# The experts' second product turned round: w2's tiles as weights, 512 tokens moving, gate weights at the relu

## The chip, the core and the metric

The kernel runs on one core of a Trainium2 chip. The metric is the device time of one execution in microseconds (us); a kernel's time is the median of its runs. Some executions also carry a profile, from which all durations below come.

## What is computed

Three networks follow each other. The first is a linear recurrence over 768 time steps (4 batches, 8 heads of 48 features); its output, as 3072 tokens of 384 features, is the x of a mixture of 8 experts. Its output in turn goes through a layer with h x cos(h).

```python
def _moe_ref(x, w_gate, w1, w2):          # N, D, E, F = 3072, 384, 8, 1024
    logits = x @ w_gate
    P = np.exp(logits - logits.max())
    for _ in range(8):
        P /= P.sum(1, keepdims=True) + 1e-09
        P /= P.sum(0, keepdims=True) + 1e-09
        P *= N / E
    out = np.zeros((N, D))
    for e in range(E):
        h = np.maximum(x @ w1[e], 0.0)
        out += P[:, e:e + 1] * (h @ w2[e])
    return out

def _moe2_ref(x, w_in, w_out):            # d_ff = 2048
    h = x @ w_in
    return (h * np.cos(h)) @ w_out
```

## The kernel before

**Units, blocks, steps.** Both dense networks are cut into units of 256 hidden columns (FU): four a expert (UPE), 32 for the experts (NU1), eight more for the second network (40, NU). The tokens are cut into six blocks of 512 (TB, NTB), a block into four tiles of 128 (TPB). One `step(u, tb)` does a unit for a block, in two halves f = 0, 1. Every value is split into a high and a low part (hh and hl, xh and xl, wh and wl), and a product is three matmuls, high x high, high x low and low x high (`three`, L288).

**g1 and g2.** `g1` (L340) makes a hidden tile of 128 hidden features by 512 tokens: three 128-deep slices of w1 are the weights, xh and xl of the block move, nine matmuls of 512 columns into a PSUM bank. `relu_split` (L293) writes hh with ScalarE and hl with VectorE, both from the bank. `g2` (L358) multiplies with w2: weights are 128 tokens of hh or hl, w2's 384 columns move; six matmuls give one token tile of 384 features. A half of a step holds one g1 and two g2 of the step before, by the queue `g2q`. `evac` (L320) adds the bank to the accumulator `acc`, which lies as token by feature; for experts 1 to 7 one VectorE operation multiplies by the token's gate weight P on the way (L326), for expert 0 (units 0 to 3), whose weight is not known yet, plain sums are kept and scaled in unit 4 by ScalarE (L370).

**Stages and order.** 24 chunks of attention come first (loop at L682), with units 0 and 1 laid between their parts as filler: each chunk pulls `one()` twice, and a pull is half of a step's half (a g1, or the g2's behind it). Then units 2 to 39 run. `gate_tasks` (L545) computes P beside units 0 to 3, one piece a pull; weights are loaded and split by `weight_tasks` (L275) the same way, with wl on GpSimd. `to_moe2` (L603) turns the accumulator into the second network's x beside units 31 and 32: four TensorE transposes into a bank, then ScalarE (xh) and VectorE (xl). PSUM has eight banks: two for g1 (`ps1`), two to five for g2 (`ps2`), and X0, X1, X2, used by attention, gate and transposes in turn; X0 and X1 join the rings at block 4 of unit 32. The order on each engine is that of the code; nothing reorders it.

Of the kernel before, what the change touches and what calls it, by code (L numbers as in the profile page):

```python
# [9 lines left out]
F32 = mybir.dt.float32  # L10
# [4 lines left out]
ALU = mybir.AluOpType  # L15
# [52 lines left out]
def setup(tc, ap, big, psp):  # L68
# [5 lines left out]
    def sb(name, cols, dt=F32):  # L74
        return big.tile([128, cols], dt, name=name)
# [9 lines left out]
    t.accb = [sb(f"acc{i}", TPB * DM) for i in range(NTB)]  # L85
    t.acc = [t.accb[i // TPB][:, i % TPB * DM:(i % TPB + 1) * DM] for i in range(NTT)]
# [21 lines left out]
    t.wp = sb("wp", 8 * HP)[0:112].rearrange("p (i j o) -> p i j o", i=8, o=1)  # L108
    t.ps = [psp.tile([128, 512], F32, name=f"ps{i}") for i in range(8)]
# [95 lines left out]
def body(tc, ap, t, fast, branch=None):  # L205
    nc = tc.nc
    te, act, dve, pool, sp = nc.tensor, nc.scalar, nc.vector, nc.gpsimd, nc.sync
    acc, P, xh, xl = t.acc, t.P, t.xh, t.xl
# [84 lines left out]
    def relu_split(ps, hh, hl):  # L293
        act.activation(out=hh, in_=ps, func=AF.Relu)  # L294
        dve.scalar_tensor_tensor(out=hl, in0=ps, scalar=0.0, in1=hh.bitcast(F32), op0=ALU.max, op1=ALU.subtract)  # L295
# [23 lines left out]

    def evac(u, tt, ps):  # L320
        if u == 0:
            act.activation(out=acc[tt], in_=ps, func=AF.Copy)
        elif u < UPE:
            dve.tensor_tensor(out=acc[tt], in0=ps, in1=acc[tt], op=ALU.add)
        elif u < NU1:
            dve.scalar_tensor_tensor(  # L326
                out=acc[tt], in0=ps, scalar=P[:, tt, u // UPE:u // UPE + 1], in1=acc[tt], op0=ALU.mult, op1=ALU.add)
        elif u == NU1:
            act.activation(out=acc[tt], in_=ps, func=AF.Copy, scale=TWO_PI)
        else:  # L330
            dve.scalar_tensor_tensor(  # L331
                out=acc[tt], in0=ps, scalar=TWO_PI, in1=acc[tt], op0=ALU.mult, op1=ALU.add)
            if u == NU - 1:
                sp.dma_start(out=ap["out"][tt * 128:(tt + 1) * 128, :], in_=acc[tt])
# [5 lines left out]
    def g1(u, tb, f):  # L340
        assert (u, 1) in wdone
        wh, wl = t.wh[u % 2], t.wl[u % 2]
        hh, hl = hid[u, tb, f] = hring.next()
        ps = ps1.next()
        for k in range(KT):
            o = k * FU + f * 128
            three(ps, wh[:, o:o + 128], wl[:, o:o + 128], xh[tb][:, k], xl[tb][:, k], k == 0, k == KT - 1)
        return (relu_split if u < NU1 else cos_split)(ps, hh, hl)
# [8 lines left out]

    def g2(u, tb, i):  # L358
        ps = ps2.next()[:, 0:DM]
        for f in range(2):  # L360
            g2_part(u, tb, i, f, ps)
        evac(u, tb * TPB + i, ps)

    def step(u, tb, lag=0):

        if u == UPE:
            assert not gq
            for i in range(TPB):
                tt = tb * TPB + i
                act.activation(out=acc[tt], in_=acc[tt], func=AF.Copy, scale=P[:, tt, 0:1])  # L370
        for f in range(2):
            rest = g1(u, tb, f)
            yield
            if len(g2q) > lag:
                a, b, i = g2q.popleft()
                g2(a, b, i)
                g2(a, b, i + 1)
            if rest:
                rest()
            if f == 1:  # L380
                g2q.extend([(u, tb, 0), (u, tb, 2)])
            yield
# [219 lines left out]

    def to_moe2(tb):  # L603

        yield
        for k in range(KT):
            ps = (X0, X1)[(tb * KT + k) % 2]
            for i in range(TPB):
                te.transpose(  # L609
                    ps[:, i * 128:(i + 1) * 128], acc[tb * TPB + i][:, k * 128:(k + 1) * 128], t.ident)  # L610
            act.activation(out=xh[tb][:, k], in_=ps, func=AF.Copy, scale=1.0 / TWO_PI)
            dve.scalar_tensor_tensor(  # L612
                out=xl[tb][:, k], in0=ps, scalar=1.0 / TWO_PI, in1=xh[tb][:, k].bitcast(F32),
                op0=ALU.mult, op1=ALU.subtract)
            yield
# [109 lines left out]
    for u in range(2, NU):  # L725
        if u == UPE:
            while gq:
                pull(gq)
            ps2.items.append(X2)
        for tb in range(NTB):  # L730
            if tb == (1 if u + 1 < NU1 else 0) and u + 1 < NU:
                wq.append(weight_tasks(u + 1))
            if u == NU1 - 1 and tb >= 2:
                xq.append(to_moe2(tb - 2))
            if u == NU1 and tb in (0, 2):
                xq.append(to_moe2(NTB - 2 + tb // 2))
            if u == NU1 and tb == 4:
                assert not xq
                ps1.items.append(X0)
                ps2.items.append(X1)  # L740
            dense.append(Step(u, tb, lag=1 if u >= NU1 else 0))
            while one():
                pass

    late.popleft()(True)
    u, tb, i = g2q.popleft()
    while len(g2q) >= 2:
        g2(u, tb, i)
        g2(u, tb, i + 1)
        u, tb, i = g2q.popleft()  # L750
# [8 lines left out]
def program(tc, ap):  # L759
    nc = tc.nc  # L760
    with ExitStack() as stack:
# [3 lines left out]
        t = setup(tc, ap, big, psp)  # L765
# [77 lines left out]
```

## Time and profile before

| | us |
|---|---|
| median of 3 runs (2151.34 to 2154.53) | 2152.92 |
| profiled execution, its own time | 2150.08 |
| its span | 2148.3 |
| TensorE busy | 2130.2 |
| VectorE busy | 1118.8 |
| ScalarE busy | 651.1 |
| GpSimd busy | 434.7 |

The profile names TensorE PE (its weight loads PEld), VectorE DVE, ScalarE ACT, GpSimd POOL, and SyncE's DMA queue SPq. The busy time of pipelined matmuls is modelled and runs over into the next; how fast TensorE goes is read from the distance between two starts. The granted clock was 0.996 of full speed over the span. Lines (L289) are those of the kernel before.

### The profile page before, as it was taken

Reading aid. Unit: us, or ns where it says so; the run is one execution under the profiler, and the core shown is the slowest. Engines: PE = TensorE matmul, PEld = TensorE weight load, DVE = VectorE, ACT = ScalarE, POOL = GpSimd, SP = SyncE. Lnnn points to the kernel's source line nnn. Section 1 sums busy time; section 2 is a strip of 40 time slices with the busy share of each in tenths; the row PEclk is TensorE's granted clock in tenths of the full one; section 3 lists DMA queues with packets and bytes.
Section 4 is the critical chain, followed back from the end, with each engine's and each line's share of the span. In section 5 each row is a group of like instructions: output and inputs, shape, how many; then the busy total and the mean of one; then the engine's idle time right before and its main releaser. Section 6 shows DMA issues by size and latency. Waiting matters only on the chain.

```text
span 2148.3 us, 29906 instructions
## 1 busy us (share of the span) xinstructions
PE 2130.2 (99%) x12229; PEld 1910.7 (89%) x12229; DVE 1118.8 (52%) x1980; ACT 651.1 (30%) x1246; POOL 434.7 (20%) x404
## 2 busy tenths in 40 slices
PE   8999999999999999999999999999999999999998
PEld 6887889999999999999999999999999989999998
DVE  8553654444444444444444444444444676777775
ACT  4553123111111111111111111111111267666664
POOL 8872000000000000000000000000000024444442
PEclk8999999999999999999999999999999999999999
DMA  7441000000000000000000000000000001110002
GB/s 227 135 143 36 23 15 15 15 16 19 19 19 19 15 16 15 16 15 16 15 15 16 15 19 19 16 19 19 16 15 23 23 23 33 35 30 30 30 23 91
DMA packets 37331, 70.79 MB, mean 33 GB/s; under 512 B 4416, under 2 KB 27328, under 8 KB 37184
## 3 DMA queue, kind: packets, MB, share of 16 engines
q1 hardware_dynamic: 37184, 68.78, 10.6%
q8 instruction: 98, 1.61, 0.3%
q14 instruction: 49, 0.40, 0.1%
HBM read 64.04 MB, written 4.72 MB: 32 GB/s over the span
## 4 chain that ended last, share of the span: by engine, by line
PE 97%; DVE 1%; DMA 1%; ACT 0%; issue 0%; SPq 0%; DVEq 0%
PE ps L289 31%; PE ps L291 31%; PE ps L290 31%; PE ps L461 1%; PE ps L502 1%; PE ps L510 1%; PE ps L528 0%; DMA raw<-in_rkT_dram 0%; PE ps L609 0%; DMA st<-in_wpk_dram 0%; PE ps L556 0%; PE ps L557 0%; DVE xl L612 0%; ACT raw L307 0%; ACT raw L308 0%
## 5 line engine op out<-in xcount | busy, mean ns | idle before, releaser
L295 DVE SCALAR_TENSOR_TENSOR hl<-ps,hh 128x512 fp32r<-128x512 f32 x384 | 266.1, 693 | 773.0 <-ACT hh L294 772.9
L289 PE MATMUL ps<-wh,hh 128*128 128x384 f32 x1920 | 649.4, 338 | 0.0
L291 PE MATMUL ps<-wh,hl 128*128 128x384 f32 x1920 | 647.8, 337 | 0.0
L290 PE MATMUL ps<-wl,hh 128*128 128x384 f32 x1920 | 644.9, 336 | 0.0
L294 ACT ACTIVATE hh<-ps 128x512 fp32r<-128x512 f32 x384 | 230.1, 599 | 1265.0 <-PE ps L291 1264.8
L291 PE MATMUL ps<-xh,wl 128*128 128x512 f32 x1440 | 569.5, 395 | 0.0
L290 PE MATMUL ps<-xl,wh 128*128 128x512 f32 x1440 | 568.3, 395 | 0.0
L289 PE MATMUL ps<-xh,wh 128*128 128x512 f32 x1440 | 564.3, 392 | 0.7 <-DVE raw L311 0.7
L326 DVE SCALAR_TENSOR_TENSOR acc<-ps,P,acc 128x384 f32<-128x384 f32 x672 | 410.9, 613 | 83.3 <-PE ps L291 83.3
L267 POOL TENSOR_TENSOR wl<-st,wh 128x384 fp32r<-128x384 f32 x120 | 121.8, 1015 | 1351.3 <-PE ps L291 1298.5
L289 PEld LDWEIGHTS ps<-wh,hh 128*128 128x128 f32 x1920 | 360.8, 188 | 21.4
L290 PEld LDWEIGHTS ps<-wl,hh 128*128 128x128 f32 x1920 | 360.5, 188 | 19.5
L291 PEld LDWEIGHTS ps<-wh,hl 128*128 128x128 f32 x1920 | 360.1, 188 | 0.0
L291 PEld LDWEIGHTS ps<-xh,wl 128*128 128x128 f32 x1440 | 270.0, 187 | 58.1
L289 PEld LDWEIGHTS ps<-xh,wh 128*128 128x128 f32 x1440 | 270.6, 188 | 48.3 <-issue 3.0
L290 PEld LDWEIGHTS ps<-xl,wh 128*128 128x128 f32 x1440 | 270.1, 188 | 45.2
L315 POOL TENSOR_TENSOR hl<-raw,hh 128x512 fp32r<-128x512 f32 x95 | 140.7, 1481 | 209.5 <-ACT hh L314 110.6
L304 DVE SCALAR_TENSOR_TENSOR raw<-raw,ps 128x512 f32<-128x512 f32 x96 | 66.0, 688 | 72.7 <-ACT raw L303 72.7
L303 ACT ACTIVATE raw<-ps,magic 128x512 f32<-128x512 f32 x96 | 66.1, 689 | 102.1 <-PE ps L291 100.8
L331 DVE SCALAR_TENSOR_TENSOR acc<-ps,acc 128x384 f32<-128x384 f32 x168 | 87.8, 551 | 4.9 <-PE ps L291 4.9
L311 DVE SCALAR_TENSOR_TENSOR raw<-raw,ps 128x512 f32<-128x512 f32 x96 | 66.0, 688 | 20.2 <-ACT raw L308 20.2
L307 ACT ACTIVATE raw<-raw 128x512 f32<-128x512 f32 x96 | 61.0, 636 | 24.9 <-DVE raw L304 24.9
(134 smaller groups left out, 1013.8 us busy)
## 6 DMA issues: line engine op xcount, KB each, us to landing
st<-in_wpk_dram SPq DMA_DIRECT2D x128, 192.0 KB, 2.4
AM<-in_wpk_dram SPq DMA_DIRECT2D x32, 384.0 KB, 3.0
raw<-in_rkT_dram SPq DMA_DIRECT2D x21, 448.0 KB, 3.6
kr<-in_kr_dram SPq DMA_DIRECT2D x21, 384.0 KB, 4.1
v<-in_v_dram SPq DMA_DIRECT2D x21, 224.0 KB, 4.5
out_dram<-acc SPq DMA_DIRECT2D x24, 192.0 KB, 1.9
acc<-in_rkT_dram SPq DMA_DIRECT2D x3, 448.0 KB, 3.9
acc<-in_kr_dram SPq DMA_DIRECT2D x3, 384.0 KB, 4.6
```

The costliest lines, as they stand in the source:

```text
L267: (dve if u < 2 else pool).tensor_tensor(out=wl[:, s], in0=src, in1=wh[:, s].bitcast(F32), op=ALU.subtract)
L289: te.matmul(ps, ah, bh, start=first, stop=False)
L290: te.matmul(ps, ah, bl, start=False, stop=False)
L291: te.matmul(ps, al, bh, start=False, stop=last)
L294: act.activation(out=hh, in_=ps, func=AF.Relu)
L295: dve.scalar_tensor_tensor(out=hl, in0=ps, scalar=0.0, in1=hh.bitcast(F32), op0=ALU.max, op1=ALU.subtract)
L303: act.activation(out=f, in_=ps, func=AF.Identity, bias=t.magic)
L304: dve.scalar_tensor_tensor(out=f, in0=f, scalar=MAGIC, in1=ps, op0=ALU.subtract, op1=ALU.subtract)
L311: dve.scalar_tensor_tensor(out=f, in0=f, scalar=0.5, in1=ps, op0=ALU.subtract, op1=ALU.mult)
L315: (dve if last else pool).tensor_tensor(out=hl, in0=f, in1=hh.bitcast(F32), op=ALU.subtract)
L326: dve.scalar_tensor_tensor(out=acc[tt], in0=ps, scalar=P[:, tt, u // UPE:u // UPE + 1], in1=acc[tt], op0=ALU.mult, op1=ALU.add)
L331: dve.scalar_tensor_tensor(out=acc[tt], in0=ps, scalar=TWO_PI, in1=acc[tt], op0=ALU.mult, op1=ALU.add)
```

## The change

Three things change. First, g2 for the experts becomes `g2T`: a 128x128 slice of w2 is the weight, hh and hl of the block move with 512 columns, and a bank holds 128 output features by 512 tokens. Three such products (k = 0, 1, 2) replace four, and they are queued as one in the first half and two in the second. The accumulator lies as feature by token (`accT`) until unit 32.

Second, a token's gate weight now differs along the columns. It is applied to the hidden tile: for experts 1 to 7 VectorE writes h = max(ps, 0) x pb, ScalarE copies it to hh, VectorE subtracts. `pb` holds an expert's gate weights of a block on all 128 partitions; P is transposed (two TensorE transposes), written to DRAM, and loaded back with broadcast, twelve loads ahead of unit 4 and six in each expert's last unit. Expert 0's sum is multiplied by `pb0` on GpSimd in unit 4.

Third, `to_moe2` needs no transposes, and X0, X1 and X2 join the rings at unit 4 (one more bank for g1, two for g2).

```diff
-    def relu_split(ps, hh, hl):
+    hring32 = Ring([x[:, 0:TB] for x in t.v[0:3]])
+    def relu_split(e, tb, ps, hh, hl):
+        if e:
+            h = hring32.next()
+            dve.scalar_tensor_tensor(out=h, in0=ps, scalar=0.0, in1=t.pb[tb], op0=ALU.max, op1=ALU.mult)
+            act.activation(out=hh, in_=h, func=AF.Copy)
+            dve.tensor_tensor(out=hl, in0=h, in1=hh.bitcast(F32), op=ALU.subtract)
+            return
...
+    def evacT(u, tb, k, ps):
+        a = accT[tb][:, k]
+        if u == 0:
+            act.activation(out=a, in_=ps, func=AF.Copy)
+        else:
+            dve.tensor_tensor(out=a, in0=ps, in1=a, op=ALU.add)
...
+    def g2T(u, tb, k):
+        wh, wl = t.wh[u % 2], t.wl[u % 2]
+        ps = ps2.next()
+        for f in range(2):
+            hh, hl = hid[u, tb, f]
+            o = KT * FU + f * DM + k * 128
+            three(ps, wh[:, o:o + 128], wl[:, o:o + 128], hh, hl, f == 0, f == 1)
+        evacT(u, tb, k, ps)
...
+    def load_pb(e, tb):
+        row = (e * NTB + tb) * TPB
+        sp.dma_start(
+            out=t.pb0[tb] if e == 0 else t.pb[tb],
+            in_=t.pT[row:row + TPB, :].rearrange("t p -> (t p)").partition_broadcast(128))
...
         if u == UPE:
-            for i in range(TPB):
-                tt = tb * TPB + i
-                act.activation(out=acc[tt], in_=acc[tt], func=AF.Copy, scale=P[:, tt, 0:1])
+            pool.tensor_tensor(
+                out=accT[tb], in0=accT[tb],
+                in1=t.pb0[tb].rearrange("p (o n) -> p o n", o=1).to_broadcast([128, KT, TB]), op=ALU.mult)
         for f in range(2):
             rest = g1(u, tb, f)
+            if f == 1 and u >= UPE and (u + 1) % UPE == 0 and u + 1 < NU1:
+                load_pb((u + 1) // UPE, tb)
...
-                g2q.extend([(u, tb, 0), (u, tb, 2)])
+                g2q.extend([(u, tb, (0,)), (u, tb, (1, 2))] if u < NU1 else [(u, tb, (0, 1)), (u, tb, (2, 3))])
...
+        for i in range(2):
+            te.transpose(X2[0:half, i * 128:(i + 1) * 128], m[:, i * half:(i + 1) * half], t.ident)
...
+            sp.dma_start(out=t.pT[i * half:(i + 1) * half, :], in_=pt[:, i])
+        for tb in range(NTB):
+            load_pb(1, tb)
+            load_pb(0, tb)
     def to_moe2(tb):
         for k in range(KT):
-            ps = (X0, X1)[(tb * KT + k) % 2]
-            for i in range(TPB):
-                te.transpose(
-                    ps[:, i * 128:(i + 1) * 128], acc[tb * TPB + i][:, k * 128:(k + 1) * 128], t.ident)
-            act.activation(out=xh[tb][:, k], in_=ps, func=AF.Copy, scale=1.0 / TWO_PI)
+            act.activation(out=xh[tb][:, k], in_=accT[tb][:, k], func=AF.Copy, scale=1.0 / TWO_PI)
...
-            ps2.items.append(X2)
+            ps1.items.append(X0)
+            ps2.items.extend([X1, X2])
```

On TensorE, in a steady step of the experts, this is the product that stands between two hidden tiles; a row reads bank, moving operand, weights and size (ps are the PSUM banks, numbered over the whole program). Before, the second half:

```order
L289 MATMUL ps_126<-wh_87,hh_97 128x384 [waits DVE_49]
L290 MATMUL ps_126<-wl_89,hh_97 128x384
L291 MATMUL ps_126<-wh_87,hl_98 128x384
L289 MATMUL ps_126<-wh_87,hh_99 128x384
L290 MATMUL ps_126<-wl_89,hh_99 128x384
L291 MATMUL ps_126<-wh_87,hl_100 128x384
L289 MATMUL ps_129<-wh_87,hh_97 128x384 [waits DVE_49]
L290 MATMUL ps_129<-wl_89,hh_97 128x384
L291 MATMUL ps_129<-wh_87,hl_98 128x384
```

After, the last matmuls of the hidden tile in a second half, and the first of its two products:

```order
L296 MATMUL ps_130<-xl_79,wh_90 128x512
L297 MATMUL ps_130<-xh_73,wl_92 128x512
L295 MATMUL ps_132<-hh_99,wh_90 128x512
L296 MATMUL ps_132<-hl_100,wh_90 128x512
L297 MATMUL ps_132<-hh_99,wl_92 128x512
L295 MATMUL ps_132<-hh_101,wh_90 128x512
L296 MATMUL ps_132<-hl_102,wh_90 128x512
L297 MATMUL ps_132<-hh_101,wl_92 128x512
```

Weights and moving operand have changed places, and all rows of a step now have 512 columns.

On VectorE, the same place: first before, one hl and two evacuations in each half,

```order
L295 SCALAR_TENSOR_TENSOR hl_98<-ps_122,hh_97 128x512 [waits Activation_49]
L326 SCALAR_TENSOR_TENSOR acc_83<-ps_124,P,acc_83 128x384 [waits PE_49]
L326 SCALAR_TENSOR_TENSOR acc_83<-ps_125,P,acc_83 128x384 [waits PE_49]
L295 SCALAR_TENSOR_TENSOR hl_100<-ps_123,hh_99 128x512 [waits Activation_49]
L326 SCALAR_TENSOR_TENSOR acc_83<-ps_126,P,acc_83 128x384 [waits PE_49]
L326 SCALAR_TENSOR_TENSOR acc_83<-ps_129,P,acc_83 128x384 [waits PE_49]
```

and after (v are the buffers of h, raw those of the gate weights pb):

```order
L304 SCALAR_TENSOR_TENSOR v_111<-ps_130,raw_103 128x512 [waits DMAHW5_49,PE_49]
L306 TENSOR_TENSOR hl_100<-v_111,hh_99 128x512 [waits Activation_49]
L339 TENSOR_TENSOR acc_83<-ps_128,acc_83 128x512 [waits PE_49]
L304 SCALAR_TENSOR_TENSOR v_109<-ps_125,raw_103 128x512 [waits PE_49]
L306 TENSOR_TENSOR hl_102<-v_109,hh_101 128x512 [waits Activation_49]
L339 TENSOR_TENSOR acc_83<-ps_129,acc_83 128x512 [waits PE_49]
L339 TENSOR_TENSOR acc_83<-ps_131,acc_83 128x512 [waits PE_49]
```

VectorE now has two operations around ScalarE's copy, and reads h and hh for hl where it read the bank; three evacuations of 512 columns stand where four of 384 stood.

On GpSimd, at unit 4, after (before, only the L267 rows, the splits of weights, stand there):

```order
L273 TENSOR_TENSOR wl_91<-st_94,wh_89 128x384 [waits DMAHW0_49,PE_49,Activation_49]
L399 TENSOR_TENSOR acc_83<-acc_83,AM_119 128x1536 [waits DMAHW4_49,DVE_49]
L399 TENSOR_TENSOR acc_84<-acc_84,AM_119 128x1536 [waits DMAHW6_49,DVE_49]
L273 TENSOR_TENSOR wl_92<-st_93,wh_90 128x384 [waits DMAHW7_49,PE_49,Activation_49]
L273 TENSOR_TENSOR wl_92<-st_94,wh_90 128x384 [waits DMAHW0_49,PE_49,Activation_49]
L399 TENSOR_TENSOR acc_85<-acc_85,AM_120 128x1536 [waits DVE_49]
```

The six multiplications of expert 0's sum (AM, RB and Z hold pb0) have come from ScalarE to GpSimd, between the splits for unit 5.

## Rows read from the trace of the kernel before

**Rows 1.** The page: busy time by engine, and the chain that ended last.

```profile
PE 2130.2 (99%) x12229; PEld 1910.7 (89%) x12229; DVE 1118.8 (52%) x1980; ACT 651.1 (30%) x1246; POOL 434.7 (20%) x404
PE 97%; DVE 1%; DMA 1%; ACT 0%; issue 0%; SPq 0%; DVEq 0%
```

**Rows 2.** Busy time in three windows: length, then each engine's us, clock, DMA.

```profile
60.00:100.00 40.00, 40.00 (x567) 33.55 (x566) 19.61 (x37) 21.31 (x62) 37.03 (x39) 1.00 0.41 125
900.00:950.00 50.00, 50.00 (x253) 45.29 (x252) 22.00 (x36) 8.64 (x16) 4.04 (x4) 1.00 0.06 16
1710.00:1718.40 8.40, 8.40 (x48) 7.67 (x48) 6.70 (x13) 2.01 (x5) 0.00 (x0) 1.00 0.15 47
```

**Rows 3.** Timeline of TensorE, one half of a step: start us, us, operation.

```profile
1001.75 0.39 PE L289 MATMUL ps<-xh,wh 128*128 128x512 f32 x1
...
1003.83 0.33 PE L289 MATMUL ps<-wh,hh 128*128 128x384 f32 x1
...
1004.89 0.33 PE L289 MATMUL ps<-wh,hh 128*128 128x384 f32 x1
...
1005.93 0.39 PE L289 MATMUL ps<-xh,wh 128*128 128x512 f32 x1
```

**Rows 4.** Timeline of TensorE: hidden tile starts, first and last, 324 halves apart.

```profile
319.32 0.39 PE L289 MATMUL ps<-xh,wh 128*128 128x512 f32 x1
...
1675.80 0.39 PE L289 MATMUL ps<-xh,wh 128*128 128x512 f32 x1
```

**Rows 5.** Timeline of TensorE around the transposes; in brackets, the wait before.

```profile
1726.25 0.60 PE L609 MATMUL ps<-ident,acc 128*128 128x128 f32 x4
1726.61 0.48 PE L289 MATMUL ps<-xh,wh 128*128 128x512 f32 x1
1726.92 0.40 PE L290 MATMUL ps<-xl,wh 128*128 128x512 f32 x1
...
1739.81 0.50 PE L289 MATMUL ps<-xh,wh 128*128 128x512 f32 x1 [0.74 <-DVE raw L311]
...
1756.42 0.66 PE L609 MATMUL ps<-ident,acc 128*128 128x128 f32 x4 [0.71 <-DVE xl L612]
```

**Rows 6.** Groups of instructions: count | busy us, mean ns | idle before and releaser.

```profile
L326 DVE SCALAR_TENSOR_TENSOR acc<-ps,P,acc 128x384 f32<-128x384 f32 x672 | 410.9, 613 | 83.3 <-PE ps L291 83.3
L295 DVE SCALAR_TENSOR_TENSOR hl<-ps,hh 128x512 fp32r<-128x512 f32 x384 | 266.1, 693 | 773.0 <-ACT hh L294 772.9
...
L315 POOL TENSOR_TENSOR hl<-raw,hh 128x512 fp32r<-128x512 f32 x95 | 140.7, 1481 | 209.5 <-ACT hh L314 110.6 <-issue 84.9 <-DVE kr L255 9.7
...
L314 ACT ACTIVATE hh<-raw 128x512 fp32r<-128x512 f32 x96 | 59.8, 623 | 2.8 <-DVE raw L311 2.8
...
L324 DVE TENSOR_TENSOR acc<-ps,acc 128x384 f32<-128x384 f32 x72 | 39.4, 554 | 14.6 <-PE ps L291 14.3
...
L430 DVE TENSOR_TENSOR kr<-kr,urep 128x384 f32<-128x384 f32 x5 | 5.8, 1158 | 0.2
```

**Rows 7.** Timeline of ScalarE and of VectorE, one operation each.

```profile
1004.03 0.60 ACT L294 ACTIVATE hh<-ps 128x512 fp32r<-128x512 f32 x1 [3.59 <-PE ps L291]
...
2138.19 0.69 DVE L315 TENSOR_TENSOR hl<-raw,hh 128x512 fp32r<-128x512 f32 x1 [0.77 <-ACT hh L314]
```

**Rows 8.** Lines L599 and L370 (first and last start), and a window as in rows 2.

```profile
L599 DVE SCALAR_TENSOR_TENSOR P<-P,RB x8: 357/359/645, 245.7 to 291.1; 128x192 f32<-128x192 f32 x8
...
L370 ACT ACTIVATE acc<-acc,P x24: 602/607/609, 317.9 to 361.3; 128x384 f32<-128x384 f32 x24
...
0.00:20.00 20.00, 14.32 (x126) 12.93 (x126) 17.18 (x35) 7.34 (x21) 16.22 (x30) 0.83 0.83 254
```

**Rows 9.** Timeline of VectorE and TensorE in an attention chunk: Z written, Z read.

```profile
137.07 0.73 DVE L542 TENSOR_TENSOR Z<-ps,Z 48x192 f32<-48x192 f32 x2
...
138.02 0.84 PE L510 MATMUL ps<-raw,Z 112*32 112x128 f32 x24
```

## What I expect of the change

> **What bounds the kernel now.** I read the page's busy times first, then its chain, then stretches of the span, then single matmuls. TensorE is busy 99% of the span and makes 97% of the chain that ended last [rows 1]. The reader is to see that no stage is left in which something else bounds: in a steady stretch of the experts (900 to 950 us), in the attention stretch (60 to 100 us) and late in the experts (1710 to 1718.4 us) TensorE is busy for the whole window, at a granted clock of 1.00, the 2.4 GHz level [rows 2]. VectorE is busy 22.0 of 50 us in the steady stretch, ScalarE 8.6, GpSimd 4.0. So only what TensorE streams, and what could make it wait, moves the end.
>
> A step (one unit of 256 hidden columns for one block of 512 tokens) is two halves. In a half, nine matmuls of 512 columns make a hidden tile and twelve of 384 columns multiply earlier hidden tiles by w2 [rows 3]. The nine take from 1001.75 to 1003.83, 2.08 us. The twelve take from 1003.83 to 1005.93: the last six 1.04 us (173 ns each), the first six 1.06 us. From the first start to the last of [rows 4] lie 324 halves in 1356.48 us, 4.187 us each. Averaged over these halves the nine take 2.081 us and the twelve 2.106 us.
>
> **The product itself (gain, 9.9 us).** The change turns twelve matmuls of 384 columns in a half into nine of 512 on average (six in one half, twelve in the next). The columns are the same, 4608; there are three matmuls and three weight loads fewer. The nearest row to the new form is the nine of the hidden product: same width, weights also 128x128 slices of w, moving operand also a 512-wide token tile. So I put nine of the new ones at 2.081 us against 2.106, which gives 0.0257 us in a half; 32 units x 6 blocks x 2 = 384 halves give 9.9 us. The bounds are 0 and 9.9. At the low end: 173.3 ns for 384 columns and 231.2 ns for 512 are both 0.451 ns a column, so the steady rate goes by columns alone, and the 0.026 us sit only in the first six behind each hidden tile. If what slows those six follows the new product, nothing is gained. I take the upper end, because the nine that follow a g2 product show no such surplus.
>
> The Trainium skill's TensorE: Matmul & The Clock Gate, section Back-to-back issue gap, prices this otherwise: a warm matmul takes columns/2.4 ns and a constant of 2.5 ns. By that constant the term would be an estimated 2.9 us (1152 matmuls fewer). The rows (231 and 173 ns) are longer than its 216 and 163 ns.
>
> **The transposes between the two networks (gain, 7.9 us).** The accumulator is now feature by token, so the 72 transposes at L609 go, in 18 groups of four. A group takes 0.36 us (1726.25 to 1726.61), and the matmul behind it 0.31 us instead of 0.23 [rows 5]: 0.44 us x 18 = 7.9 us, all on the path, since TensorE does not wait around them.
>
> **Two waits (gain, 1.5 us).** TensorE waits 0.74 us at 1739.81 for the second hidden bank and 0.71 us at 1756.42 for the transpose bank [rows 5]. The hidden product gets a third bank from unit 4 on (before, from block 4 of unit 32), and the transpose banks are not used as such any more. Both waits go; what is late next there is VectorE, below.
>
> **Two passes on VectorE instead of one (0.5 us, bounds 0 and 4).** For experts 1 to 7 the relu becomes: VectorE h = max(ps,0) x gate, ScalarE copy to hh, VectorE hl = h - hh. Prices: h 0.69 us (as L295), the copy 0.62 us (as L314) [rows 6], hl 0.69 us (the one VectorE L315) [rows 7]. ScalarE starts 0.2 us after the next product began (1003.83 in [rows 3], 1004.03 in [rows 7]); so hh and hl are there some 2.3 us after the hidden product ended. The hidden tile of the second half is read first after two w2 column tiles (12 x 0.231 = 2.78), the next hidden product (2.08) and three matmuls (0.69): 5.55 us. The cover is 3.2 us. VectorE's sum in a step is 4 x 0.69 + 3 x 0.69 for the three wider evacuations = 4.8 us, against 2 x 0.69 + 4 x 0.61 = 3.8 us before, in 8.3 us. Behind the wait of hl for ScalarE (about 0.7 us) only evacuations are queued, and their five banks come round after five products, over 10 us.
>
> The tightest place is unit 31, where VectorE also converts weights and writes xl: 6.70 of 8.40 us [rows 2]. There I take out four evacuations (4 x 0.61 = 2.45) and put in three wider ones and two h (5 x 0.69 = 3.45): 7.7 us, plus two waits of 0.7: 9.1 us in a step of 8.33. That is 0.8 us too much in each of four steps (blocks 2 to 5), 3.1 us, just under the cover of 3.2. I take a cost of 0.5 us, bounds 0 and 4.
>
> **GpSimd at unit 4 (0.3 us, bounds 0 and 7).** Six multiplications of 128x1536 replace 24 small ScalarE scalings that cost nothing. One is three times L315 on GpSimd, 3 x 1.48 = 4.4 us [rows 6]. The evacuation that needs the product comes a step (8.3 us) later. The row that speaks against it is L430: a VectorE operation with two SBUF operands of 384 columns took 1.16 us beside a busy GpSimd, while L324 of the same width from PSUM took 0.55 us [rows 6]. hl is now such an operation. A delay of 0.6 us stays under the cover of 3.2. The bound: an hl that had to wait for a whole multiplication would be 4.4 us late, 1.2 more than the cover, six times at most, 7 us. The Trainium skill's SBUF — State Buffer, section Who interferes with whom, says that a VectorE instruction with two SBUF inputs and a GpSimd instruction that reads SBUF exclude each other, the later one waiting until the other ends, which would be that bound; L430 agrees in direction, with 0.6 us.
>
> **The gate table (0.3 us).** Two transposes more, at 0.36/4 us each plus the change of form; a table goes to DRAM and comes back as twelve loads of 256 KB. The last gate operation starts at 291.1 us, four pulls of the work list (2.1 us each) lie before the loads, so they are issued from about 300 us; unit 4 starts at 317.9 [rows 8]. 3.1 MB at the 254 GB/s of the first 20 us [rows 8] take 12 us, and each later block needs its pair 8.3 us later than the one before. SP's queue holds nothing urgent there. The reloads at each expert's last unit wait on SP for h alone and are used a unit (50 us) later; the weight pieces behind them have most of a unit. Cost nothing.
>
> **Attention (0.5 us, bounds 0 and 3).** The filler between two chunks is now 6 or 12 matmuls of 512 instead of 12 of 384. Z is ready at 137.80 and read from 138.02 [rows 9]: 0.22 us of cover, of which a wider evacuation ahead on VectorE takes 0.14 (0.69 against 0.55). Ten chunks have that evacuation; each may lose up to 0.3 us.
>
> **Sum.** Gains 9.9 + 7.9 + 1.5 = 19.3; costs 0.5 + 0.3 + 0.3 + 0.5 = 1.6; net 17.7 us. The profiled execution's own time is 2150.08 us (span 2148.3), which gives 2132.4. The median of the runs is 2152.92, 0.13% above it; from that, 2135.2 us, the forecast.
>
> **Rivals.** (A) The surplus of the first six stays, whoever causes it: 7.9 + 1.5 - 1.6 = 7.8, 2145.1 us. For it: it appears behind every hidden tile alike. Against it: no surplus in the nine. (B) What is saved is a constant per matmul: 8.6 ns if the whole 25.7 ns of a half belong to its three matmuls, 0 by the last six; halfway, 4.3 ns x 1152 = 5.0 us instead of 9.9, 2140.1 us. For it: only the means over twelve. The Trainium skill's section named above is a rule of this kind, with a smaller constant. (C) Stalls at the two seams, unit 4 and unit 31, at their bounds: 3 to 7 us more, about 2140 us. For it: VectorE over its step in unit 31. (D) The other side: the longer relu chain outgrows its cover in the steady step. Its place is the first read of the second half's hidden tile; its price is the overrun in each of 28 x 6 = 168 steps. It decides from 17.7/168 = 0.105 us of overrun on, that is a chain of 5.65 us instead of 2.3; at 0.2 us it adds 33.6, 2168.8 us. Against it: the chain would have to be more than twice the sum of its rows.
>
> **How the numbers follow.** Forecast 0.52, A 0.16, B 0.06, C 0.18, D 0.08. The likeliest gives 2135.2. The range reaches from the full gain without any cost, 2133.6, less half the spread of the runs (1.6), to A with 1.9 us of C: 2132.0 to 2147.0. Faster by over 0.2% (4.3 us, about what a measurement of this kernel can tell from no change): forecast, A, B and C but for a joint A and C, 0.84; within 0.2%: 0.08; slower: 0.08.
>
> **What would show it.** Right: no TensorE wait between units 5 and 30, each half 4.162 us long, no surplus behind the hidden tile, 18 gaps less around the seam of the networks. Wrong: steps still of 8.37 us (A); TensorE waiting for hl in every step (D), or only at unit 4 behind GpSimd or in unit 31 behind VectorE (C); loads of the gate table landing after 318 us.

## The result and the profile after

The changed kernel takes 2115.02 us (median of 4 runs, 2112.90 to 2118.71), the kernel before 2152.13 beside it: a ratio of 0.983, interval 0.9809 to 0.985. The gain is 37 us, twice the forecast's 17.7, and the time lies below the range. The profiled execution's own time is 2112.90 us, 37.2 below the 2150.08 of before.

Page of the changed kernel: busy time, and the chain that ended last (answers [rows 1]).

```profile
PE 2085.6 (99%) x11007; PEld 1742.3 (83%) x11007; DVE 1284.2 (61%) x2132; ACT 648.3 (31%) x1216; POOL 465.6 (22%) x410
PE 94%; DVE 3%; ACT 1%; DMA 1%; issue 1%; POOL 0%; SPq 0%; ACTq 0%; DVEq 0%; POOLq 0%
```

TensorE still bounds; VectorE now has 3% of the chain. Windows of the changed kernel, columns as in [rows 2]; the second is units 31 and 32, where experts and second network meet ("the seam" below).

```profile
900.00:950.00 50.00, 50.00 (x222) 41.40 (x221) 28.19 (x43) 9.84 (x17) 4.42 (x4) 1.00 0.11 30
1639.98:1746.70 106.72, 99.69 (x452) 82.67 (x451) 81.90 (x143) 54.93 (x100) 21.18 (x18) 1.00 0.09 26
```

TensorE's timeline after, one step: hidden product, one w2 tile, hidden product, two w2 tiles (answers [rows 3]). The lines are now L295 to L297.

```profile
1003.50 0.39 PE L295 MATMUL ps<-xh,wh 128*128 128x512 f32 x1
...
1005.54 0.39 PE L295 MATMUL ps<-hh,wh 128*128 128x512 f32 x1
...
1006.90 0.39 PE L295 MATMUL ps<-xh,wh 128*128 128x512 f32 x1
...
1008.95 0.39 PE L295 MATMUL ps<-hh,wh 128*128 128x512 f32 x1
```

The nine matmuls of a hidden product take 2.04 us, where they took 2.08: code that the change did not touch became faster. All matmuls of 512 columns now start 226.7 ns apart, in g1 and in g2T.

The starts of units 4, 31, 32 and 33 after (the first two answer [rows 4]), and then of units 32 and 33 before:

```profile
318.07 0.39 PE L295 MATMUL ps<-xh,wh 128*128 128x512 f32 x1
...
1639.98 0.39 PE L295 MATMUL ps<-xh,wh 128*128 128x512 f32 x1
...
1693.00 0.39 PE L295 MATMUL ps<-xh,wh 128*128 128x512 f32 x1
...
1746.70 0.39 PE L295 MATMUL ps<-xh,wh 128*128 128x512 f32 x1
```

```profile
1731.32 0.39 PE L289 MATMUL ps<-xh,wh 128*128 128x512 f32 x1
...
1784.12 0.39 PE L289 MATMUL ps<-xh,wh 128*128 128x512 f32 x1
```

| stretch | before, us | after, us | difference |
|---|---|---|---|
| start to unit 4 | 319.32 | 318.07 | -1.25 |
| units 4 to 30 | 1356.48 | 1321.91 | -34.57 |
| units 31 and 32 | 108.32 | 106.72 | -1.60 |
| unit 33 to the end of the own time | 365.96 | 366.20 | +0.24 |

So nearly the whole gain lies in the steady experts, where a half went from 4.187 to 4.080 us, and the seam, where 7.9 us of transposes left TensorE, is hardly shorter. There TensorE waits (after; answers [rows 5]):

```profile
1686.88 0.50 PE L295 MATMUL ps<-hh,wh 128*128 128x512 f32 x1 [2.37 <-ACT hh L305]
...
1696.72 0.50 PE L295 MATMUL ps<-hh,wh 128*128 128x512 f32 x1 [0.84 <-ACT hh L305]
...
1709.13 0.44 PE L295 MATMUL ps<-wh,hh 128*128 128x384 f32 x1 [1.54 <-ACT hh L328]
...
1710.49 0.44 PE L297 MATMUL ps<-wh,hl 128*128 128x384 f32 x1 [0.73 <-POOL hl L329]
```

Measured as starts that come late against the steady distance, TensorE loses 9.7 us in these two units: 3.9 behind the relu's hh and hl in unit 31, 1.6 behind them at the start of unit 32 (1696.72), and 4.2 behind the hh and hl of cos (L328, L329).

### The profile page after: what moved, and what is told of

It is laid out like the page before. It is cut to its first block, busy times and chain, and to the rows that moved or that the text cites. A ratio compares the mean times of both kernels' runs of the same rounds, so it can differ in the third digit from the quotient of the medians.

```text
span 2111.0 us, 27533 instructions
## 1 busy us (share of the span) xinstructions
PE 2085.6 (99%) x11007; PEld 1742.3 (83%) x11007; DVE 1284.2 (61%) x2132; ACT 648.3 (31%) x1216; POOL 465.6 (22%) x410
## 4 chain that ended last, share of the span: by engine, by line
PE 94%; DVE 3%; ACT 1%; DMA 1%; issue 1%; POOL 0%; SPq 0%; ACTq 0%; DVEq 0%; POOLq 0%
PE ps L295 30%; PE ps L297 30%; PE ps L296 30%; PE ps L535 1%; PE ps L494 1%; PE ps L543 1%; DMA raw<-in_rkT_dram 1%; DVE xl L657 0%; DVE acc L339 0%; PE ps L561 0%; ACT hh L305 0%; DVE hl L306 0%; DVE v L304 0%; DMA st<-in_wpk_dram 0%; PE ps L589 0%
## 5 line engine op out<-in xcount | busy, mean ns | idle before, releaser
L295 PE MATMUL ps<-xh,wh 128*128 128x512 f32 x1440 | 564.0, 392 | 0.0
L297 PE MATMUL ps<-xh,wl 128*128 128x512 f32 x1440 | 562.5, 391 | 0.0
L295 PE MATMUL ps<-hh,wh 128*128 128x512 f32 x1152 | 450.6, 391 | 3.2 <-ACT hh L305 3.2
L296 PE MATMUL ps<-hl,wh 128*128 128x512 f32 x1152 | 448.7, 389 | 0.7 <-DVE hl L306 0.7
L297 PE MATMUL ps<-hh,wl 128*128 128x512 f32 x1152 | 448.4, 389 | 0.0
L304 DVE SCALAR_TENSOR_TENSOR v<-ps,raw 128x512 f32<-128x512 f32 x336 | 232.1, 691 | 326.7 <-PE ps L297 326.7
L339 DVE TENSOR_TENSOR acc<-ps,acc 128x512 f32<-128x512 f32 x558 | 378.6, 686 | 18.2 <-PE ps L297 17.8
L306 DVE TENSOR_TENSOR hl<-v,hh 128x512 fp32r<-128x512 f32 x336 | 233.6, 695 | 254.5 <-ACT hh L305 254.5
L295 PEld LDWEIGHTS ps<-xh,wh 128*128 128x128 f32 x1440 | 270.3, 188 | 57.0 <-issue 3.0
L297 PEld LDWEIGHTS ps<-xh,wl 128*128 128x128 f32 x1440 | 270.2, 188 | 57.1
L295 PEld LDWEIGHTS ps<-hh,wh 128*128 128x128 f32 x1152 | 216.2, 188 | 50.1 <-ACT hh L305 4.5
L296 PEld LDWEIGHTS ps<-hl,wh 128*128 128x128 f32 x1152 | 216.3, 188 | 46.0 <-DVE hl L306 1.6
L297 PEld LDWEIGHTS ps<-hh,wl 128*128 128x128 f32 x1152 | 216.2, 188 | 45.0
L329 POOL TENSOR_TENSOR hl<-raw,hh 128x512 fp32r<-128x512 f32 x95 | 140.0, 1474 | 205.0 <-ACT hh L328 110.0
L297 PE MATMUL ps<-wh,hl 128*128 128x384 f32 x384 | 129.8, 338 | 1.6 <-POOL hl L329 1.6
L295 PE MATMUL ps<-wh,hh 128*128 128x384 f32 x384 | 129.5, 337 | 1.5 <-ACT hh L328 1.5
L296 PE MATMUL ps<-wl,hh 128*128 128x384 f32 x384 | 129.0, 336 | 0.0
```

The costliest lines, as they stand in the source:

```text
L295: te.matmul(ps, ah, bh, start=first, stop=False)
L296: te.matmul(ps, ah, bl, start=False, stop=False)
L297: te.matmul(ps, al, bh, start=False, stop=last)
L304: dve.scalar_tensor_tensor(out=h, in0=ps, scalar=0.0, in1=t.pb[tb], op0=ALU.max, op1=ALU.mult)
L306: dve.tensor_tensor(out=hl, in0=h, in1=hh.bitcast(F32), op=ALU.subtract)
L329: (dve if last else pool).tensor_tensor(out=hl, in0=f, in1=hh.bitcast(F32), op=ALU.subtract)
```

## The experiments

Two questions stood: why a half lost 107 ns instead of 26, and where the transposes' 7.9 us went.

### The product: e1, e2, e3, e10, e4

Two theories. W: a matmul costs its columns at 2.4 GHz plus a constant, and a half in which widths change costs a surplus. R: the new form, or the new operands, have a rate of their own.

**e1.** The kernel before, with g2 moving 512 columns (384 of w2 and 128 more), so that all widths are equal and the form is the old one.

```diff
-        three(ps, hh[:, s], hl[:, s], wh[:, o:o + DM], wl[:, o:o + DM], f == 0, f == 1)
+        n = TB if u < NU1 else DM
+        three(ps[:, 0:n], hh[:, s], hl[:, s], wh[:, o:o + n], wl[:, o:o + n], f == 0, f == 1)
...
```

> The kernel before, but the experts' second product moves 512 columns of w instead of 384 (128 columns that nobody reads are added; weights are still the hidden tiles). Theory W (width): a matmul costs columns/2.4 GHz plus 13.3 ns, and what comes on top of it in the kernel before (66 ns in a half step) is the price of alternating 384 and 512 columns. Then all 21 matmuls of a half take 226.7 ns, also the nine of the hidden product: 4.76 us a half, 384 halves x 0.573 us more than before, 2372 us. Theory R (roles): the surplus comes from loading hidden tiles as weights, whatever the width. Then the hidden product stays at 231 ns, 4.83 us a half, 2398 us.

2379.59 us (before 2148.84). TensorE's timeline, first start of g2's twelve and of g1's nine:

```profile
702.54 0.39 PE L291 MATMUL ps<-xh,wh 128*128 128x512 f32 x1
...
704.58 0.39 PE L291 MATMUL ps<-wh,hh 128*128 128x512 f32 x1
```

g1's nine take 2.04 us here too, with the old product between them. A half is 4.760 us, 21 times 226.7 ns, as theory W has it (the time is 8 us above W's figure; the excess lies before unit 2). So neither form nor operands matter, nor the banks, which are those of before; equal widths do.

**e2 and e3.** The kernel after, with the experts' g2T on only 384 of 512 tokens (e2, below), and with g1 cut to 384 in the same way as well (e3).

```diff
...
-            three(ps, wh[:, o:o + 128], wl[:, o:o + 128], hh, hl, f == 0, f == 1)
+            three(ps[:, 0:DM], wh[:, o:o + 128], wl[:, o:o + 128], hh[:, 0:DM], hl[:, 0:DM], f == 0, f == 1)
```

> The changed kernel, but its second product moves only the first 384 of the 512 tokens of a block (the last 128 are left out of the product). Widths alternate again, roles are those of the changed kernel. W: the hidden product goes back from 226.7 to 231 ns and the first 384-column matmuls behind it show a surplus: 3.67 us a half in the steady experts, about 1956 us and what the seams add. R: the hidden product stays at 226.7, the others take 173.3, 3.60 us a half, about 1931 us and seams.

> The changed kernel with both products of the experts at 384 columns (128 of 512 tokens left out of both). One width again, a narrower one. W with its constant of 13.3 ns: every matmul takes 173.3 ns, 3.12 us a half, about 1746 us and seams. If instead a stream of one width simply runs at a better rate per column (0.443 ns as in the changed kernel, no constant): 170.0 ns, 3.06 us a half, about 1723 us and seams.

e2: 1957.87 us. TensorE's timeline, a g1, a g2T of six matmuls, the next g1:

```profile
700.69 0.39 PE L297 MATMUL ps<-xh,wh 128*128 128x512 f32 x1
...
702.77 0.33 PE L297 MATMUL ps<-hh,wh 128*128 128x384 f32 x1
...
703.84 0.39 PE L297 MATMUL ps<-xh,wh 128*128 128x512 f32 x1
```

The widths alternate again, and the surplus is back in the new form: a mean of 231.2 ns for g1 and 176.2 for g2T, units of 44.00 us, which is 66 ns a half above 9 x 226.7 + 9 x 173.3. e3: 1767.33 us. A g1, a g2T of twelve, the next g1:

```profile
700.61 0.33 PE L297 MATMUL ps<-xh,wh 128*128 128x384 f32 x1
...
702.17 0.33 PE L297 MATMUL ps<-hh,wh 128*128 128x384 f32 x1
...
704.25 0.33 PE L297 MATMUL ps<-xh,wh 128*128 128x384 f32 x1
```

Equal widths of 384: every matmul 173.3 ns apart, units of 37.44 us, no surplus. The time of e3 is above its figure because units 31 and 32 took 105.05 us, as long as in the kernel after though TensorE had less to do; that belongs to the second question.

**e10.** The kernel before, with g2 on 256 of w2's 384 columns in the experts.

```diff
...
-        three(ps, hh[:, s], hl[:, s], wh[:, o:o + DM], wl[:, o:o + DM], f == 0, f == 1)
+        n = 256 if u < NU1 else DM
+        three(ps[:, 0:n], hh[:, s], hl[:, s], wh[:, o:o + n], wl[:, o:o + n], f == 0, f == 1)
```

> The kernel before, but in the 32 units of the experts g2 moves only 256 of w2's 384 columns (a third of the output is left out), so the widths that alternate are 512 and 256. Theory W (columns at 2.4 GHz and a constant of 13.3 ns a matmul, and a surplus of 66 ns in a half in which the width changes): 9 x 226.7 + 12 x 120.0 + 66 = 3.546 us a half against 4.187, 384 halves: 246 us less than before, 1904. If the surplus grows with the difference in width (256 columns instead of 128): 132 ns a half, 1930. Rival L (a matmul cannot follow faster than its weights are loaded, which takes longer than 120 ns here): g2's pitch stays near 170 ns, 2120.

1893.90 us, 10 below theory W. TensorE's timeline, a g1, the g2 behind it, the next g1:

```profile
700.29 0.40 PE L291 MATMUL ps<-xh,wh 128*128 128x512 f32 x1
...
702.35 0.28 PE L291 MATMUL ps<-wh,hh 128*128 128x256 f32 x1
...
703.79 0.40 PE L291 MATMUL ps<-xh,wh 128*128 128x512 f32 x1
```

From the second to the last of the twelve, starts are 120.0 ns apart: the constant holds at a third width (120.0 - 106.7 = 13.3 ns), and loading the weights sets no floor at 120 ns. The surplus did not grow with the difference in width, as one rival had it: over the steady units the nine take 2.067 us, 229.7 ns each and 27 ns too much, and the twelve 1.433 us, 7 ns too little (all in the first step), together 20 ns a half. So its size does not follow from the widths by any rule that I have; only that it needs two widths is shown.

**e4.** The kernel before, with both g1 of a step ahead of its 24 g2 matmuls in units 3 to 30: the same matmuls, half as many changes of width.

```diff
+            grouped = 2 < u < NU1 - 1
+            for _ in range(2 * f if grouped else 1):
+                if len(g2q) > lag:
+                    a, b, i = g2q.popleft()
+                    g2(a, b, i)
+                    g2(a, b, i + 1)
```

> The kernel before, but in units 3 to 30 a step does both hidden products first (18 matmuls of 512) and then all four products with w2 (24 of 384), so widths change half as often. If the surplus is paid at each change of width: half of 66 ns x 336 halves, 11 us less, about 2141 us, with surplus in the first six of 24 only. If it is paid by each matmul as long as both widths are in the stream: no change, about 2152 us, hidden product still at 231 ns throughout.

2151.89 us: by the time alone, no change, which speaks for the rival. The trace speaks otherwise. TensorE's timeline of a step: two nines of g1, the first six of g2, the other eighteen.

```profile
638.57 0.39 PE L289 MATMUL ps<-xh,wh 128*128 128x512 f32 x1
...
640.65 0.39 PE L289 MATMUL ps<-xh,wh 128*128 128x512 f32 x1
...
642.69 0.33 PE L289 MATMUL ps<-wh,hh 128*128 128x384 f32 x1
...
643.75 0.33 PE L289 MATMUL ps<-wh,hh 128*128 128x384 f32 x1
...
646.88 0.39 PE L289 MATMUL ps<-xh,wh 128*128 128x512 f32 x1
```

The first nine take 2.08 us, the second nine 2.04; the first six of g2 1.06, the other eighteen 3.13, or 174 ns each. A step takes 8.307 us against 2 x 4.187: one surplus of 66 ns instead of two, 49.84 us a unit instead of 50.24, 10.8 us over units 4 to 30. The total doesn't show it because this execution reached unit 3 at 273.53 us instead of 267.83 (the code up to there is unchanged), and unit 3 took 6.2 us longer, with TensorE waiting for the gate's sums (3.1 us) and once for an evacuation (1.6 us), and running at the 1.2 GHz level for some 3 us behind the first of these waits. So the surplus belongs to the change of width, and lies in the first nine 512s and first six 384s behind it. What in the change makes it, these runs don't show.

### The seam: e6, e7, e5, e8, e9, e11, e12

**e6.** The kernel after, with the one-pass relu for all experts (the gate weights of experts 1 to 7 are left out of the result), all matmuls as they are.

```diff
-            return relu_split(u // UPE, tb, ps, hh, hl)
+            return relu_split(0, tb, ps, hh, hl)
```

> The changed kernel with the old one-pass relu for all experts (ScalarE and VectorE read the bank; the gate weights of experts 1 to 7 are left out). W: the pitch in the steady experts stays at 226.7 ns; VectorE has 24 operations less in unit 31, so the loss at the seam shrinks: 2104 to 2108 us. Theory P (the surplus came from ScalarE's reading of the bank beside TensorE's writing): the pitch goes back to 231 ns, 336 halves x 0.066 to 0.106 us, 2130 us or more.

2106.25 us. All that TensorE still waits for in units 31 and 32 (line waited for: us in total, times, longest):

```profile
PE ps L297 <- POOL hl L329: 1.6, 3, 0.7
```

Units 4 to 30 are as long as after, 1321.92 us, so the steady gain owes nothing to the relu. Units 31 and 32 take 99.59 us instead of 106.72. Unit 31 has no loss left (48.96 us), so it is the relu's chain of passes that TensorE waits for there. VectorE has 12 operations less in that unit (one a half, not the 24 of the expectation), so this run doesn't tell the chain from VectorE's load.

**e7.** The kernel after, with the 72 transposes put back into `to_moe2` (into banks of g2's ring; nobody reads them).

```diff
+            ps = ps2.next()
+            for i in range(TPB):
+                te.transpose(ps[:, i * 128:(i + 1) * 128], accT[tb][:, k, i * 128:(i + 1) * 128], t.ident)
```

> The changed kernel with the 72 transposes put back as work that nobody reads (into a bank of the second product's ring). By the rows of before they cost 18 x 0.44 = 7.9 us on TensorE: 2123 us. If they fall into the time that TensorE waits at the seam anyway: less, 2115 to 2119 us.

2116.21 us, not 2123. Window 1680 to 1690 us, first after, then e7 (columns as in [rows 2]):

```profile
1680.00:1690.00 10.00, 7.41 (x31) 5.55 (x31) 7.60 (x14) 3.18 (x6) 1.00 (x1) 1.00 0.13 40
```

```profile
1680.00:1690.00 10.00, 10.00 (x52) 8.24 (x51) 7.44 (x13) 2.75 (x6) 1.01 (x1) 1.00 0.12 40
```

TensorE is full again and units 31 and 32 take 106.87 us, 0.15 more than without the transposes. Removing them gained nothing here: without them TensorE spends their time waiting.

**e5.** Theory V said that VectorE has too much to do in unit 31. The kernel after, with unit 31's hl on GpSimd:

```diff
-            dve.tensor_tensor(out=hl, in0=h, in1=hh.bitcast(F32), op=ALU.subtract)
+            (pool if u == NU1 - 1 else dve).tensor_tensor(out=hl, in0=h, in1=hh.bitcast(F32), op=ALU.subtract)
...
```

> The changed kernel, with hl of unit 31 (12 subtractions) on GpSimd instead of VectorE. Units 31 and 32 took 111.5 us in the changed kernel against 99.2 without any wait (48.96 and 50.24 for a steady unit of either kind), so 12.3 us are lost there. If VectorE's queue is what is late in unit 31 (theory V: its work and its waits for ScalarE are over 8.2 us in a step): 12 x 0.6 us of work and 12 waits of 0.76 us leave its queue, most of the 12.3 us go, 2104 to 2108 us. If ScalarE's queue or the transfers of the second network's weights are late there: no change, 2115 us.

2115.03 us (2113.50 to 2117.31; 0.9834 of before, interval 0.9818 to 0.985), units 31 and 32 107.82 us: no gain. (The expectation's 111.5 us for these units after was a wrong reading; the starts above give 106.72.) GpSimd is the slower engine for it (1.29 us an hl against 0.69), and TensorE now waits for `POOL hl L306` (1.4 us). Between 1690 and 1700 us TensorE's granted clock was 0.66 besides, so the run doesn't decide about V.

**e8 and e9.** The kernel after, with `to_moe2`'s xl moved from VectorE to ScalarE and GpSimd, for blocks 0 to 3 (e8) or all six (e9).

```diff
+            if tb < 4:
+                act.activation(out=accT[tb][:, k], in_=accT[tb][:, k], func=AF.Copy, scale=1.0 / TWO_PI)
+                pool.tensor_tensor(
+                    out=xl[tb][:, k], in0=accT[tb][:, k], in1=xh[tb][:, k].bitcast(F32), op=ALU.subtract)
+                yield
+                continue
```

> The kernel after, but for blocks 0 to 3 of the second network's x (written beside unit 31) the low part xl is made by ScalarE (scaling the accumulator in place) and GpSimd (the subtraction), not by VectorE: 12 of the 18 operations of 735 ns at L657 leave VectorE. In the kernel after, units 31 and 32 take 106.7 us (g1 starts 1639.98 to 1746.70) where TensorE's own work there is some 98. Theory S (VectorE holds the relu back in unit 31, by its load of 8.4 us in 10 and by its waits for ScalarE's xh): most of unit 31's share goes, units 31 and 32 take 99 to 103 us, time 2107 to 2111. Rival T (the relu's three passes on three in-order engines are the delay, whatever else VectorE does): stays at 106 to 107, time 2113 to 2117. Rival U (GpSimd and ScalarE become late for unit 32): slower than 2117.

> As the run with blocks 0 to 3, but all six blocks, so also the two that are written beside unit 32, where ScalarE is busy 8.5 us of 10 (1720 to 1750 us of the kernel after). Theory S: unit 32 (53.7 us in the kernel after) gets no longer, time within 2 us of that run. Rival U: ScalarE is the late one in unit 32, each of its six added copies of 0.62 us shows there: 2 to 4 us longer than that run.

e8: 2113.15 us (2112.63 to 2114.16; 0.9829, interval 0.9813 to 0.9846), units 31 and 32 106.53 us. e9: 2112.63 us, 106.99. Unit 32 took 53.5 and 53.9 us, so rival U's 2 to 4 us did not come. By the times theory T would hold. But TensorE's waits fell from 7.0 to 4.7 us in e8, and the clock took what that gained. Windows of e8:

```profile
1680.00:1685.00 5.00, 4.10 (x18) 2.97 (x16) 3.31 (x6) 3.15 (x6) 3.15 (x3) 1.00 0.23 79
1685.00:1690.00 5.00, 4.11 (x11) 3.16 (x11) 4.78 (x7) 0.90 (x3) 1.72 (x2) 0.66 0.00 0
```

From 1686.38 to 1689.37 us, behind waits of 0.90 and 0.90, matmuls of 512 columns start 0.43 us apart: the 1.2 GHz level. The same happens again from 1710.48 to 1713.67 us, behind waits of 1.54 and 0.73 (384 columns 0.32 us apart); late starts cost 1.6 us in each of the two stretches. So these two runs do not settle whether VectorE's load is the cause.

**e11.** What the trace of after shows in unit 31 is an order, not a load. VectorE, ScalarE and GpSimd there (start, us, operation, and in brackets the wait before):

```profile
1682.77 0.55 DVE L261 SCALAR_TENSOR_TENSOR kr<-kr,kr 128x384 f32<-128x384 f32 x1
1684.44 1.07 DVE L657 SCALAR_TENSOR_TENSOR xl<-acc,xh 128x512 fp32r<-128x512 f32 x1 [1.11 <-ACT xh L656]
1685.43 0.68 DVE L304 SCALAR_TENSOR_TENSOR v<-ps,raw 128x512 f32<-128x512 f32 x1
1686.86 0.69 DVE L306 TENSOR_TENSOR hl<-v,hh 128x512 fp32r<-128x512 f32 x1 [0.76 <-ACT hh L305]
```

```profile
1683.36 0.52 ACT L272 ACTIVATE wh<-kr 128x384 fp32r<-128x384 f32 x1 [2.37 <-DVE kr L261]
1683.79 0.62 ACT L656 ACTIVATE xh<-acc 128x512 fp32r<-128x512 f32 x1
1686.20 0.63 ACT L305 ACTIVATE hh<-v 128x512 fp32r<-128x512 f32 x1 [1.79 <-DVE v L304]
```

```profile
1683.96 1.00 POOL L273 TENSOR_TENSOR wl<-kr,wh 128x384 fp32r<-128x384 f32 x1 [12.09 <-ACT wh L272]
```

ScalarE's wh waits for VectorE's last conversion step (L261); xh is queued behind wh; VectorE's xl waits for xh; the relu's h (L304) is queued behind xl; ScalarE's hh waits for h; and TensorE waits 2.37 us for hh. Two queues that run in order wait for each other in turn. A smaller part is not order: this xl took 1.07 us where others take 0.68, because it began beside GpSimd's wl and ended 0.55 us behind it (last section). e11 is the kernel after, with xl (issued by `low`) one piece of the work list later than its xh:

```diff
             act.activation(out=xh[tb][:, k], in_=accT[tb][:, k], func=AF.Copy, scale=1.0 / TWO_PI)
+            if k:
+                low(k - 1)
             yield
+        low(KT - 1)
```

> The kernel after, but VectorE's xl is issued one piece of the work list later than ScalarE's xh of the same slice; VectorE's work is the same. In the kernel after VectorE waits 6.7 us for xh at L657 in units 31 and 32, with the relu's h queued behind it. Theory O (it is this order that makes the relu late): units 31 and 32 take 99 to 103 us instead of 106.7, time 2107 to 2111. Rival Q (it is VectorE's load, which is unchanged): 106 to 107, 2113 to 2117.

2108.31 us (2106.44 to 2109.94; 0.9803, interval 0.9787 to 0.9819). Units 31 and 32 take 102.05 us, with VectorE's work unchanged. VectorE's wait for xh in these units after, and the largest wait that it has there in e11 (columns as in e6):

```profile
DVE xl L657 <- ACT xh L656: 6.7, 6, 1.9
```

```profile
DVE hl L306 <- ACT hh L305: 9.1, 12, 0.8
```

The first is gone in e11; the second stood there after too, with the same 9.1 us. Theory O holds. The gain isn't that of fewer collisions with GpSimd: in e11 two xl beside GpSimd's hl took 1.8 us each, which is more than after lost by its two (1.19 and 1.07 us).

**e12.** In e11, the relu's hl is also issued behind the next pieces of the work list instead of directly behind h.

```diff
...
-            dve.tensor_tensor(out=hl, in0=h, in1=hh.bitcast(F32), op=ALU.subtract)
-            return
+            return lambda: dve.tensor_tensor(out=hl, in0=h, in1=hh.bitcast(F32), op=ALU.subtract)
...
             yield
+            if rest and u < NU1:
+                rest()
+                rest = None
             if len(g2q) > lag:
```

> The version in which xl is issued one piece later (2108.31 us), and in it the relu's hl is also issued behind the next pieces of the work list on VectorE (weight conversion, xl), no longer directly behind h; VectorE's work is the same. In that version VectorE still waits 9.9 us in 13 waits for ScalarE's hh at L306 between 1640 and 1750 us, and units 31 and 32 take 102.05 us, with 5.05 us of TensorE's time lost. Theory O (order: VectorE's waits for ScalarE hold the queue behind them): units 31 and 32 take 99 to 101 us, time 2105.5 to 2107.5. Rival Q2 (what is left is VectorE's load, or hl itself comes later by what is now ahead of it): 102 to 104 us, 2108 to 2111. In units 4 to 30 both expect 48.96 us a unit, as before.

2105.53 us (5 runs, 2104.47 to 2110.80; 0.9793 of before, interval 0.9775 to 0.981). All five lie below the fastest run of the kernel after; the kernel before took 2149.35 us beside it, 2.8 less than beside the kernel after, so some 7 of the 9.5 us between the two are left. Units 31 and 32 take 97.92 us, less than theory O's 99 to 101, with 1.1 us of late starts left. These units in e12 (to be read against those of after), and VectorE's waits for hh there:

```profile
1647.40:1745.32 97.92, 97.53 (x451) 82.97 (x450) 82.14 (x143) 54.44 (x100) 21.97 (x18) 1.00 0.09 29
```

```profile
DVE hl L306 <- ACT hh L305: 4.1, 8, 0.8
```

VectorE has the same 143 operations and 82 us of work as after, now in 97.92 us instead of 106.72, and TensorE doesn't wait in unit 31 any more. So it was the order and not the load.

## Why the forecast was wrong, step by step

**The product itself: the failed step.** Forecast 9.9 us with bounds 0 and 9.9; measured 34.57 in units 4 to 30 alone, 0.1067 us a half instead of 0.0257. The step went wrong where it took 231.2 ns as the steady rate of 512 columns: from "173.3 ns for 384 columns and 231.2 ns for 512 are both 0.451 ns a column" it followed that columns alone count. e10, e3 and e1 show 120.0, 173.3 and 226.7 ns for 256, 384 and 512 columns: 53.3 ns for 128 columns, 2.4 GHz, and 13.3 ns for every matmul. The equal quotients were a coincidence: 231.2 held 4.5 ns of surplus. I took the nine for free of it because they had no row beside them to differ from; every nine in the trace stood behind a product of another width. What a half gains is three matmuls x 13.3 = 40 ns, and the surplus of 66 ns (40 in the nine, 26 in the first six, the only part that I saw). Over 324 halves that is 13.0 + 21.5 = 34.5 us.

**Rival B** was right in kind, a constant per matmul, but with 4.3 ns halfway and 8.6 at most too small, and without the surplus in g1. The constant of 2.5 ns that the Trainium skill's TensorE: Matmul & The Clock Gate, section Back-to-back issue gap, gives for the isolated gap of a warm matmul does not fit this stream: the form of its rule agrees, the measured constant is 13.3 ns. Rival A (the surplus stays) fell: it needs two widths.

**The transposes and the two waits.** Forecast 7.9 + 1.5 us gained; measured 1.6 for the whole of units 31 and 32. That the work leaves TensorE was right (e12 has 10.4 us less there than before, the product's 1.3 in unit 31 included); that the path gets shorter by it was not, since the relu's chain came late at the same place (e7: putting them back costs 0.15 us). This second miss went the other way and hid a part of the first.

**Two passes on VectorE.** Forecast 0.5 us, bounds 0 and 4; measured: none in units 5 to 30, as forecast, and 9.7 us lost in units 31 and 32, 5.5 of it behind the relu and 4.2 behind cos. The step summed VectorE's work and two waits of 0.7 (9.1 us in a step of 8.33). The place was right, and rival C named it, but the size came from something the sum doesn't hold: VectorE and ScalarE waiting for each other in order. To see it, the queues of both engines had to be read row by row, not added up.

**GpSimd at unit 4.** Forecast 0.3 us, bounds 0 and 7. A multiplication takes 3.53 us (estimate 4.4), and TensorE doesn't wait in unit 4: nothing. The mechanism behind the bound is there (last section), but here no hl began early in a multiplication; that is the timing of this kernel, nothing that the forecast had worked out. The 0.6 us read from L430 was a mean too: its five operations took 0.56 to 2.21 us.

**The gate table.** Forecast 0.3 us. The loads were issued from 299.1 us and landed within 7.1 us; no wait shows behind them.

**Attention.** Forecast 0.5 us, bounds 0 and 3. It can't be read at that size: unit 4 starts at 318.07 us after, but between 317.5 and 325.5 in the profiles of e5 to e9, e11 and e12, whose code up to there is the same. One such cost I did not look for: the gate's small matmuls in units 2 and 3 now stand behind a fill of six matmuls in every other half, and twice TensorE loses 0.7 to 0.8 us for VectorE's sums (here at 246.60):

```profile
246.60 0.39 PE L628 MATMUL ps<-RB,ones 128*128 128x8 f32 x2 [0.64 <-DVE RB L625]
```

Units 2 and 3 took 105.90 us, 106.09 before, where 24 halves of 0.107 should have saved 2.6; these two waits are 1.5 of what is missing.

**Rival D** (the relu chain outgrows its cover in every step) did not come: units 4 to 30 have 48.96 us each, like e6 with the short chain.

## What to carry to other kernels

A rate per column, taken from a stream in which two widths alternate, hides what each matmul costs beside its columns, even where both widths give the same quotient: measure each width in a stretch of its own before pricing a change by columns. Work taken off the bounding engine is a gain only where its next input is ready by then, so look at what is late next as a chain through all queues. Where two in-order queues feed each other, issue the consumer a piece later than its producer; that gave 8.8 us in units 31 and 32 here, with no work removed.

## What the runs showed of the hardware

- A stream of matmuls with 128x128 weights starts one every columns/2.4 GHz plus 13.3 ns (120.0, 173.3 and 226.7 ns for 256, 384 and 512); at 512 it is the same whichever operand moves (e1 and the kernel after).
- Where 512 and 384 alternate, the first nine 512s behind the change average 231.2 ns and the first six 384s 177.6, together 66 ns, in either form (before and e2); with 256 it is 20 ns, 27 more in the 512s and 7 less in the 256s. What makes it stays open.
- After waits in unit 31 the granted clock fell to the 1.2 GHz level in e5, e8 and e9 (0.66 over 10 us, 0.66 over 5, 0.83 over 10) and not in the kernel after, whose longest wait there, 2.37 us, was longer than e8's 0.90. In unit 32 it fell in e8 behind waits of 1.54 and 0.73 us, and after not, behind the same two. The runs don't settle what decides it.
- Three times in unit 4 an hl (two SBUF inputs, VectorE) began while GpSimd was in a multiplication, and each lasted until 0.54 or 0.55 us behind the multiplication's end. GpSimd and VectorE after:

```profile
334.84 3.53 POOL L399 TENSOR_TENSOR acc<-acc,AM 128x1536 f32<-128x1536 f32 x1
343.00 3.53 POOL L399 TENSOR_TENSOR acc<-acc,AM 128x1536 f32<-128x1536 f32 x1
346.49 3.97 POOL L399 TENSOR_TENSOR acc<-acc,RB 128x1536 f32<-128x1536 f32 x1
```

```profile
338.07 0.84 DVE L306 TENSOR_TENSOR hl<-v,hh 128x512 fp32r<-128x512 f32 x1 [0.76 <-ACT hh L305]
346.24 0.84 DVE L306 TENSOR_TENSOR hl<-v,hh 128x512 fp32r<-128x512 f32 x1 [0.76 <-ACT hh L305]
349.63 1.38 DVE L306 TENSOR_TENSOR hl<-v,hh 128x512 fp32r<-128x512 f32 x1 [0.76 <-ACT hh L305]
```

The first ends at 338.91, 0.54 behind 338.37; the last at 351.01, 0.55 behind 350.46; alone an hl takes 0.69 us. The other side shows too: the third multiplication above, which began while an hl was still running, took 3.97 us instead of 3.53. The Trainium skill's SBUF — State Buffer, section Who interferes with whom, says that the later of two such operations waits until the other ends; the traces agree: the hl here began 0.29 to 0.83 us before that end, and in e11 an xl that began 0.04 us behind the start of a GpSimd operation of 1.29 us lasted 1.80 us, until 0.55 behind its end. An operation that began as early in a multiplication of 3.5 us was not met.
